# Token scales of a chunk transposed into one PSUM bank and copied once, two steps ahead of their use

## The chip, the cores and the metric

The kernel runs on one core of a Trainium2 chip. Five engines work at once and meet at semaphores: TensorE (matmuls and transposes, called PE in the profile, its weight loads PEld), VectorE (DVE), ScalarE (ACT), GpSimd (POOL) and SyncE (SP, which issues DMAs). Each engine runs its own instructions strictly in the order in which they were placed. The metric is device time in microseconds (us) of one execution.

## The reference, cut to what matters

Three layers follow each other: an attention with 32 memory slots, a mixture of 8 experts with two experts per token, and a dense layer over 2304 tokens of width 512. Only the last one and the sum of the two experts in front of it are touched here:

```
x = top2_w[:,0] * y_expert0 + top2_w[:,1] * y_expert1      # 2304 x 512
h = x @ w_in            # 512 -> 2048
g = h * cos(h)
out = g @ w_out         # 2048 -> 512
```

The kernel computes in pairs of fp16 numbers (a high part and the remainder), so each product is three matmuls: high by high, high by low, low by high. For that each token row of x is multiplied by a power of two of its own before it is split. The factor must be divided out again before the cosine, and there tokens stand along the free axis: the inverse scale of each token is therefore needed as a matrix in which every partition holds the same row of scales. That matrix is `bct`.

## The kernel before

The tokens are 18 tiles of 128. The last layer takes them in six chunks of 2, 2, 4, 4, 4 and 2 tiles (line 977). Each chunk has 16 steps, one for each block of 128 of the 2048 hidden columns; counted through, there are 96 steps, 0 to 95. The start of a chunk is called a border here: border 0 is step 0, border 1 step 16, border 2 step 32, and so on to border 5 at step 80.

What one step does (`m1`, lines 1047 to 1070): TensorE runs 12 matmuls into a bank `g` (line 1056 to 1058); VectorE scales the bank into `ty` with the scales `bct` (line 1064), and makes the argument of the sine in two further instructions (1065, 1066); ScalarE takes the sine (1067); VectorE multiplies it with the bank again (1068); ScalarE rounds that to fp16, the high part of `gT` (1069); GpSimd forms the low part (1070). `m2_` (line 1072) then multiplies `gT` with `w_out`, three steps after (`LAG = 3`): after the `g` matmuls of step u, TensorE runs the `o` matmuls of step u-3. The `g` banks are three in number (`bank_g`), so the matmuls of step u+1 need the bank that line 1068 of step u-2 has read for the last time.

What happens to a token tile t before its chunk (`comb`, line 986): two gathers by GpSimd fetch the tile's expert outputs, ScalarE and VectorE sum them, VectorE finds the largest magnitude (`mx`, tile `cmx`, line 1002), six instructions of one column follow, and ScalarE and VectorE write the two fp16 parts `chl`; a transposing DMA puts them into `x2T`. The inverse scale lies in column 2 of `cmx`. `cmx` has four buffers.

`c_bct` (line 1013) turns a tile's column of scales into rows: TensorE transposes the column, broadcast to 128 columns, into the PSUM bank `pb`, and ScalarE copies the 128 columns into `bct`. `pb` comes from `mbank`, which is one bank with one buffer, so the next tile's transpose waits until ScalarE has copied the one before.

The order of the work comes from two sources. Every piece is registered with a time by `at(...)`, and `issue` (line 95) turns the times into priorities; a scheduler that runs with a timeline of its own then places each instruction on its engine. Instructions recorded with `chain("P", ...)` keep the order in which they were recorded on TensorE. The copy of `c_bct` is not chained, so the scheduler places it on ScalarE among the sines and roundings. The times of the pieces in question are

```
        at(first[j] - 0.1 * (chunks[j][1] - t) - 1.0, c_bct, t)
```

that is, about 1 us before the chunk's first step, in the units of the plan.

Of the kernel before, what the change touches and what calls it, by code (L numbers as in the profile page):

```python
# [9 lines left out]
F32 = mybir.dt.float32  # L10
# [4 lines left out]
AF = mybir.ActivationFunctionType  # L15
# [4 lines left out]
P = 128  # L20
# [40 lines left out]
def fused_kernel(ctx, tc, phiT, qT, kv, wgn, noise, w1, w2, wi, wo, out):  # L61
    nc = tc.nc
    V, A, G, T, SP = nc.vector, nc.scalar, nc.gpsimd, nc.tensor, nc.sync
# [17 lines left out]
    def at(t, fn, *a, lead=None):  # L81
        line.append((t, len(line), fn, a, LEAD.get(fn.__name__, 0.0) if lead is None else lead))
# [18 lines left out]
    def l2k(shape, dt, name):  # L101
        return lp.tile(shape, dt, tag="l", name=name)


    def sm(shape, dt, name):
        return small.tile(shape, dt, name=name)
# [4 lines left out]
    ident = sm([P, P], F32, "ident")  # L111
# [39 lines left out]
    def pow2_scale(s, mx, tmp):  # L151

        V.tensor_scalar(tmp, mx.bitcast(I32), EXP_MASK, None, op0=OP.bitwise_and)
        V.tensor_scalar(tmp, tmp, float(TINY_BITS), -1.0, op0=OP.max, op1=OP.mult)
        V.tensor_scalar(s.bitcast(I32), tmp, float((3 + 253) << 23), None, op0=OP.add)

    def pow2_inv(r, s):
        V.tensor_scalar(r.bitcast(I32), s.bitcast(I32), -1.0, float(254 << 23), op0=OP.mult, op1=OP.add)
# [78 lines left out]
    def gated(key):  # L237

        return tc.issue_after(last[key].ins) if key in last else nullcontext()

    def chain(key, fn, *a, **kw):

        with gated(key):
            last[key] = fn(*a, **kw)  # L244
# [128 lines left out]
    def mbank(name):  # L373
        return bank("m", name)
# [437 lines left out]
    def mt(shape, dt, name, bufs=2):  # L812
        return pools["mp"].tile(shape, dt, tag=name, name=name, bufs=bufs)
# [162 lines left out]
    x2T, bct = {}, {}  # L976
    chunks = [(0, 2), (2, 4), (4, 8), (8, 12), (12, 16), (16, 18)]
    ch_of = {t: j for j, (a, b) in enumerate(chunks) for t in range(a, b)}

    cm = {}  # L980

    def c_place(t):
        j = ch_of[t]
        return j, slice((t - chunks[j][0]) * P, (t - chunks[j][0] + 1) * P)

    def comb(t):

        rows = min(YROWS, Y0 + (E - 1) * CAP + (t + 1) * P)
        y0, y1 = (l2k([P, DM], F32, f"y{k}") for k in range(2))
        for k, y in enumerate((y0, y1)):  # L990
            G.indirect_dma_start(out=y, out_offset=None, in_=yd[0:rows],
                                 in_offset=bass.IndirectOffsetOnAxis(ap=sidx[:, t, k:k + 1], axis=0))
        j, o = c_place(t)
        if t == chunks[j][0]:
            n = (chunks[j][1] - chunks[j][0]) * P
            x2T[j] = mt([P, 8, n], F16, "x2T")
            bct[j] = mt([P, n], F32, "bct")
        A.activation(y0, y0, AF.Copy, scale=cw[:, t, 0:1])
        V.scalar_tensor_tensor(y1, y1, cw[:, t, 1:2], y0, op0=OP.mult, op1=OP.add)
        mx = mt([P, 4], F32, "cmx", 4)  # L1000
        tmp = mt([P, 1], I32, "cmt")
        V.tensor_reduce(mx[:, 0:1], y1, axis=AX.X, op=OP.max, apply_absolute_value=True)
        pow2_scale(mx[:, 1:2], mx[:, 0:1], tmp)
        pow2_inv(ib[:, t:t + 1], mx[:, 1:2])
        V.tensor_scalar(mx[:, 2:3], ib[:, t:t + 1], 1.0 / (2.0 * math.pi), None, op0=OP.mult)
        V.tensor_tensor(osc[:, t:t + 1], ib[:, t:t + 1], ik, op=OP.mult)
        hl = l2k([P, 2, DM], F16, "chl")
        A.activation(hl[:, 0], y1, AF.Copy, scale=mx[:, 1:2])
        V.scalar_tensor_tensor(hl[:, 1], y1, mx[:, 1:2], hl[:, 0], op0=OP.mult, op1=OP.subtract)
        SP.dma_start_transpose(out=x2T[j][:, :, o], in_=hl.rearrange("p w d -> p (w d)"))  # L1010
        cm[t] = mx

    def c_bct(t):
        j, o = c_place(t)
        pb = mbank("pb")
        chain("P", T.transpose, pb[:, :P], cm.pop(t)[:, 2:3].to_broadcast([P, P]), ident)
        A.activation(bct[j][:, o], pb[:, :P], AF.Copy)  # L1017


    win, wout = [], []  # L1020
# [143 lines left out]
    first = {}  # L1164
    for u in range(len(units) + LAG):
        if u < len(units):
            j, f = units[u]
# [4 lines left out]
        if u >= LAG:  # L1172
            j, f = units[u - LAG]
# [3 lines left out]
    for j in range(2, len(chunks)):  # L1177
        a, b = chunks[j]
        y += [first[j - 1] + (first[j] - first[j - 1] - 20.0) / (b - a) * k for k in range(b - a)]
    for t in range(NT):  # L1180
        j = ch_of[t]
        at(y[t], comb, t)
        at(first[j] - 0.1 * (chunks[j][1] - t) - 1.0, c_bct, t)

    def next_table():
        chain("A", A.preload_act_table_set, "trig_and_small")
# [103 lines left out]
```

## Time and profile before

| what | value |
|---|---|
| median of three timed runs | 963.5 us (961.99 to 963.62) |
| the profiled execution | 956.12 us |
| its span, first to last instruction | 954.3 us |
| TensorE busy | 889.6 us (93%) |
| VectorE busy | 604.0 us (63%) |
| ScalarE busy | 467.3 us (49%) |
| GpSimd busy | 229.0 us (24%) |
| mean granted clock of TensorE | 0.971 |
| last layer (from border 0) | 558.9 us to the end |

The profile is one execution, recorded by the chip. A row of the timeline gives the start in us from the span's start, the duration, the engine, the line of the code (line 244 is the helper `chain`, so there one goes by the tile), the operation, the tiles written and read, the shapes, and in brackets how long the engine stood idle before it and what ended the wait. Matmuls overlap: a row's duration holds a tail that lies beside the next matmul, so the distance between starts says more than the duration. The shares of busy time are means over stages with different limits; what a change is worth must be read from the stage it touches.

### The profile page before, as it was taken

The page shows a single profiled execution, that of the slowest core. Times are in us where ns is not written, and L with a number is a line of the kernel's source. Part 1 is how long each engine was busy: PE and PEld are TensorE (multiplying, and loading weights), DVE is VectorE, ACT ScalarE, POOL GpSimd, SP SyncE. Part 2 cuts the span into 40 slices and gives each one's busy share as a digit, 9 for nine tenths or more (in the row PEclk, how much of TensorE's full clock was granted, in tenths as well). Part 3 has the DMA queues.
Part 4 walks back from the last instruction along what each step waited for, and adds up shares of the span by engine and source line. Part 5 has one row for each costly group of instructions (what it writes and reads, how often), then busy time and mean ns, then how long its engine had stood idle before and what let it go on. Part 6 is the DMA issues. An engine that isn't in the chain of part 4 may idle for free. (4 is left out here: it accounts for less than half of the span.)

```text
span 954.3 us, 14114 instructions
## 1 busy us (share of the span) xinstructions
PE 889.6 (93%) x5316; PEld 514.4 (54%) x5316; DVE 604.0 (63%) x1336; ACT 467.3 (49%) x826; POOL 229.0 (24%) x244
## 2 busy tenths in 40 slices
PE   5988179999999999999999999989999999999997
PEld 4756055564747565665746566654444444444564
DVE  4799781365866566676763458776855664555464
ACT  3575603566666666677782334443422532422242
POOL 1354831111110101011000134433421522221222
PEclk8997679999999999999999999999999999999999
DMA  9962219849887869988663363312300420200010
GB/s 355 399 255 77 78 49 271 271 159 287 273 238 252 210 263 291 282 243 314 226 188 134 100 223 76 97 37 64 91 1 12 122 44 1 78 12 1 1 45 22
DMA packets 108246, 146.54 MB, mean 154 GB/s; under 512 B 65808, under 2 KB 66448, under 8 KB 106128
## 3 DMA queue, kind: packets, MB, share of 16 engines
q1 hardware_dynamic: 89536, 103.56, 35.7%
q0 software_dynamic: 6080, 19.93, 7.2%
q10 hardware_dynamic: 12560, 22.13, 6.6%
q8 instruction: 42, 0.69, 0.3%
q14 instruction: 28, 0.23, 0.1%
HBM read 95.26 MB, written 35.13 MB: 137 GB/s over the span
## 5 line engine op out<-in xcount | busy, mean ns | idle before, releaser
L244 PE MATMUL g<-x2T,win 128*128 128x256 f16 (+1 forms) x1152 | 203.9, 327 | 0.0
L244 PE MATMUL o<-wout,gT 128*128 128x512 f16 x864 | 202.0, 379 | 0.3 <-ACT gT L1069 0.2
L244 PE MATMUL h<-x,w 128*128 128x384 f16 (+1 forms) x1440 | 201.6, 301 | 0.2 <-DVE hT L244 0.2
L244 PEld LDWEIGHTS <-w 128*128 128x128 f16 x1440 | 141.0, 99 | 56.8 <-issue 0.5
L244 PEld LDWEIGHTS <-win 128*128 128x128 f16 x1152 | 112.9, 98 | 84.0 <-issue 2.0
L1070 POOL TENSOR_TENSOR gT<-ty,gT 128x256 f16<-128x256 f32 (+1 forms) x96 | 92.0, 958 | 260.6 <-ACT gT L1069 260.4
L1067 ACT ACTIVATE tt<-tt,hp 128x256 f32<-128x256 f32 (+1 forms) x96 | 58.9, 614 | 174.8 <-DVE tt L1066 158.4
L244 PEld LDWEIGHTS <-gT 128*128 128x128 f16 x864 | 84.3, 98 | 93.1 <-ACT gT L1069 0.6
L914 PE MATMUL y<-w,hT 128*128 128x512 f16 x320 | 121.1, 379 | 2.1 <-issue 2.1
L912 PE MATMUL y<-w,hT 128*128 128x512 f16 x320 | 121.2, 379 | 0.0
L913 PE MATMUL y<-w,hT 128*128 128x512 f16 x320 | 121.1, 379 | 0.0
L1064 DVE SCALAR_TENSOR_TENSOR ty<-g,wis,bct 128x256 f32<-128x256 f32 (+1 forms) x96 | 58.9, 614 | 78.3 <-PE g L244 78.1
L244 DVE SCALAR_TENSOR_TENSOR hT<-h,hT 128x384 f16<-128x384 f32 (+1 forms) x128 | 61.3, 487 | 70.1 <-ACT hT L244 69.3
L244 ACT ACTIVATE hT<-h 128x384 f16<-128x384 f32 (+1 forms) x128 | 55.2, 435 | 88.7 <-PE h L244 56.4
L1068 DVE SCALAR_TENSOR_TENSOR ty<-g,fac,tt 128x256 f32<-128x256 f32 (+1 forms) x96 | 59.1, 615 | 51.0 <-ACT tt L1067 50.5
L244 DVE SCALAR_TENSOR_TENSOR w<-raw,wsc,w 128x1024 f16<-128x1024 f32 x56 | 70.8, 1280 | 32.0 <-ACT w L244 30.6
L1069 ACT ACTIVATE gT<-ty 128x256 f16<-128x256 f32 (+1 forms) x96 | 50.2, 523 | 59.1 <-DVE ty L1068 59.0
L851 POOL DMA_INDIRECT xg<-xd,idxB x24 | 24.9, 1036 | 222.9 <-DMA x<-xg 207.3
L1066 DVE SCALAR_TENSOR_TENSOR tt<-tt,ty 128x256 f32<-128x256 f32 (+1 forms) x96 | 64.7, 674 | 2.6
L244 ACT ACTIVATE w<-raw,wsc 128x1024 f16<-128x1024 f32 x56 | 62.5, 1139 | 2.2 <-ACT o L244 2.1
L244 ACT ACTIVATE o<-y,ysc 128x512 f32<-128x512 f32 x40 | 27.5, 686 | 70.5 <-PE y L914 70.5
L244 ACT ACTIVATE junk<-raw 128x1024 bf16<-128x1024 f32 x56 | 58.9, 1052 | 3.8 <-ACT o L244 2.9
(256 smaller groups left out, 945.1 us busy)
## 6 DMA issues: line engine op xcount, KB each, us to landing
raw<-in_w SPq DMA_DIRECT2D x32, 1024.0 KB
yd<-o ACTq DMA_DIRECT2D x40, 256.0 KB
kvt<-in_kv SPq DMA_DIRECT2D x9, 1024.0 KB
cvt<-in_wi SPq DMA_DIRECT2D x8, 1024.0 KB
wst<-cvt SPq DMA_DIRECT2D x16, 512.0 KB
cvt<-in_wo SPq DMA_DIRECT2D x8, 1024.0 KB
yd<-zero ACTq DMA_DIRECT2D x13, 512.0 KB
xd<-hl SPq DMA_DIRECT2D x18, 256.0 KB
```

The costliest lines, as they stand in the source:

```text
L244: last[key] = fn(*a, **kw)
L851: G.indirect_dma_start(out=g, out_offset=None, in_=xd[0:NA * P] if part == 0 else xd, in_offset=bass.IndirectOffsetOnAxis(ap=idx[:, col:co ...
L912: ins = [T.matmul(py, lhsT=hi[:, f, cs], rhs=w[:, 0, ws], start=(f == 0), stop=False), T.matmul(py, lhsT=hi[:, f, cs], rhs=w[:, 1, ws], st ...
L913: T.matmul(py, lhsT=hi[:, f, cs], rhs=w[:, 1, ws], start=False, stop=False),
L914: T.matmul(py, lhsT=lo[:, f, cs], rhs=w[:, 0, ws], start=False, stop=(f == 7))]
L1064: V.scalar_tensor_tensor(y, ph[:, :n], wis[:, 2 * E + c:2 * E + c + 1], bct[j], op0=OP.mult, op1=OP.mult)
L1066: V.scalar_tensor_tensor(t, t, MAGIC, y, op0=OP.subtract, op1=OP.subtract)
L1067: A.activation(t, t, AF.Sin, bias=hp, scale=-2.0 * math.pi)
L1068: V.scalar_tensor_tensor(y, ph[:, :n], fac[:, c:c + 1], t, op0=OP.mult, op1=OP.mult)
L1069: A.activation(g[:, 0, :n], y, AF.Copy)
L1070: G.tensor_tensor(g[:, 1, :n], y, g[:, 0, :n], op=OP.subtract)
```

## The change

The scales of a whole chunk go side by side into one `pb` bank (2 or 4 transposes of 128 columns), and one ScalarE instruction of 256 or 512 columns copies them. The work is registered once per chunk, at `first[j] - 5.3` in place of about `first[j] - 1.0`. `bct` is allocated there, at 512 columns, in place of in `comb` of the chunk's first tile; `cmx` has six buffers in place of four.

```
-            bct[j] = mt([P, n], F32, "bct")
...
-        mx = mt([P, 4], F32, "cmx", 4)
+        mx = mt([P, 4], F32, "cmx", 6)
...
-    def c_bct(t):
-        j, o = c_place(t)
+    def c_bct(j):
+
+        a, b = chunks[j]
         pb = mbank("pb")
-        chain("P", T.transpose, pb[:, :P], cm.pop(t)[:, 2:3].to_broadcast([P, P]), ident)
-        A.activation(bct[j][:, o], pb[:, :P], AF.Copy)
+        for t in range(a, b):
+            _, o = c_place(t)
+            chain("P", T.transpose, pb[:, o], cm.pop(t)[:, 2:3].to_broadcast([P, P]), ident)
+        bct[j] = mt([P, 512], F32, "bct")[:, :(b - a) * P]
+        A.activation(bct[j], pb[:, :(b - a) * P], AF.Copy)
...
-        at(first[j] - 0.1 * (chunks[j][1] - t) - 1.0, c_bct, t)
+        if t == chunks[j][1] - 1:
+            at(first[j] - 5.3, c_bct, j)
```

On TensorE at border 4 (step 64 starts a chunk of four tiles) the order before is: the end of step 60's `o` matmuls, four transposes, then the chunk's first `g` matmuls.

```order
L244 MATMUL o_7543<-wout_5800,gT_7874 128x512
L244 MATMUL pb_7996<-ident_73,cmx_7385 128x128
L244 MATMUL pb_7999<-ident_73,cmx_7518 128x128 [waits Activation_49]
L244 MATMUL pb_8002<-ident_73,cmx_7644 128x128 [waits Activation_49]
L244 MATMUL pb_8005<-ident_73,cmx_7766 128x128 [waits Activation_49]
L244 LDWEIGHTS win_4962 [waits DMAHW4_49,DMAHW5_49,DMAHW3_49,DMAHW2_49]
L244 MATMUL g_8008<-x2T_7381,win_4962 128x512 [waits DVE_49]
```

The same transposes in the changed kernel stand one step earlier, after step 59's `o` matmuls and ahead of step 63's `g` matmuls, which still read the chunk before (`x2T_6741`).

```order
L244 MATMUL o_7526<-wout_5797,gT_7701 128x512
L244 MATMUL pb_7945<-ident_73,cmx_7368 128x128 [waits PE_49]
L244 MATMUL pb_7945<-ident_73,cmx_7501 128x128
L244 MATMUL pb_7945<-ident_73,cmx_7627 128x128
L244 MATMUL pb_7945<-ident_73,cmx_7749 128x128
L244 LDWEIGHTS win_4964
L244 MATMUL g_7952<-x2T_6741,win_4964 128x512 [waits DVE_49]
```

The three waits on ScalarE inside the group are gone. The one wait that has come is on TensorE's own semaphore, for a matmul several hundred places before. In chunks of two tiles the group stands two steps ahead, since a step is shorter there; at border 0 it stands ahead of the last 24 `y` matmuls of the experts.

On ScalarE at the same border the copies stand before between the sine of step 63 (the row ahead of these), its rounding, the second half of a combined tile (`chl`) and the next sine.

```order
L1017 ACTIVATE bct_7382<-pb_7996 128x128 [waits PE_49]
L1017 ACTIVATE bct_7382<-pb_7999 128x128 [waits PE_49]
L1017 ACTIVATE bct_7382<-pb_8002 128x128 [waits PE_49]
L1069 ACTIVATE gT_7874<-ty_7975 128x512 [waits DVE_49]
L1008 ACTIVATE chl_8048<-y1_8032,cmx_8039 128x512 [waits DMAHW7_49,DVE_49]
L1017 ACTIVATE bct_7382<-pb_8005 128x128 [waits PE_49]
L1067 ACTIVATE tt_8022<-tt_8022,hp_98 128x512 [waits DVE_49,Activation_49]
```

In the changed kernel one copy of 512 columns stands between the sine and the rounding of step 62.

```order
L1070 ACTIVATE tt_7925<-tt_7925,hp_98 128x512 [waits DVE_49,Activation_49]
L1020 ACTIVATE bct_7950<-pb_7945 128x512 [waits PE_49]
L1072 ACTIVATE gT_7857<-ty_7924 128x512 [waits DVE_49]
L1070 ACTIVATE tt_7966<-tt_7966,hp_98 128x512 [waits DVE_49,Activation_49]
L1072 ACTIVATE gT_7857<-ty_7965 128x512 [waits DVE_49]
```

On VectorE at border 2 the search for the largest magnitude of tile 8 (`cmx_6755`) and what follows from it stand before inside step 31, the last of chunk 1, where it waits for a transpose to free one of the four `cmx` buffers.

```order
L1064 SCALAR_TENSOR_TENSOR ty_6697<-g_6684,wis_114,bct_5762 128x256 [waits PE_49,Pool_49]
L1002 TENSOR_REDUCE cmx_6755<-y1_6748 128x1 [waits PE_49]
L1065 TENSOR_SCALAR tt_6698<-ty_6697 128x256 [waits DVE_49]
L153 TENSOR_SCALAR cmt_6756<-cmx_6755 128x1 [waits DVE_49]
L1066 SCALAR_TENSOR_TENSOR tt_6698<-tt_6698,ty_6697 128x256 [waits DVE_49]
```

In the changed kernel steps 30 and 31 hold nothing but their own four instructions; those of tile 8 stand in steps 25 to 27 (at borders 3 and 4 the first tile of the chunk after next moves in the same way). In chunk 0 the four combined tiles each stand about one step later than before.

```order
L1067 SCALAR_TENSOR_TENSOR ty_6671<-g_6658,wis_114,bct_6112 128x256
L1068 TENSOR_SCALAR tt_6672<-ty_6671 128x256
L1069 SCALAR_TENSOR_TENSOR tt_6672<-tt_6672,ty_6671 128x256
L1071 SCALAR_TENSOR_TENSOR ty_6671<-g_6658,fac_159,tt_6672 128x256
L1067 SCALAR_TENSOR_TENSOR ty_6699<-g_6686,wis_114,bct_6112 128x256
L1068 TENSOR_SCALAR tt_6700<-ty_6699 128x256
```

The order of GpSimd differs by one place (one `gT` stands ahead of the second tile's gathers), that of SyncE not at all.

## Rows read from the trace of the kernel before

**Rows 1.** Who waited for whom in the last layer: total us, times, longest.

```profile
...
PE pb L244 <- ACT bct L1017: 10.0, 12, 2.2
...
```

**Rows 2.** Timeline of TensorE at border 0.

```profile
...
557.59 0.27 PE L244 MATMUL pb<-ident,cmx 128*128 128x128 f32 x1
...
558.86 0.38 PE L244 MATMUL g<-x2T,win 128*128 128x256 f16 x2
```

**Rows 3.** Timeline of all engines at border 1.

```profile
...
596.73 0.77 DVE L1066 SCALAR_TENSOR_TENSOR tt<-tt,ty 128x256 f32<-128x256 f32 x1
596.80 0.27 PE L244 MATMUL pb<-ident,cmx 128*128 128x128 f32 x1
...
598.98 0.26 ACT L1017 ACTIVATE bct<-pb 128x128 f32<-128x128 f32 x1
...
599.45 1.47 PE L244 MATMUL g<-x2T,win 128*128 128x256 f16 x12
...
```

**Rows 4.** Timeline of TensorE at border 2, and its next step.

```profile
...
639.83 0.27 PE L244 MATMUL pb<-ident,cmx 128*128 128x128 f32 x1
639.94 1.46 PE L244 MATMUL o<-wout,gT 128*128 128x512 f16 x6
...
646.35 4.11 PE L244 MATMUL g<-x2T,win 128*128 128x512 f16 x12
...
650.30 1.46 PE L244 MATMUL o<-wout,gT 128*128 128x512 f16 x6
...
651.59 2.75 PE L244 MATMUL g<-x2T,win 128*128 128x512 f16 x12
...
```

**Rows 5.** Busy time by stretch; PEclk, DMA share and GB/s stand last.

```profile
...
646.00:647.00 1.00, 0.91 (x3) 0.57 (x4) 0.66 (x1) 0.61 (x3) 0.58 (x1) 0.50 0.00 0
...
```

**Rows 6.** Timeline of TensorE at borders 3, 4 and 5.

```profile
...
726.70 0.27 PE L244 MATMUL pb<-ident,cmx 128*128 128x128 f32 x1
...
729.23 1.02 PE L244 MATMUL g<-x2T,win 128*128 128x512 f16 x4
...
812.11 0.27 PE L244 MATMUL pb<-ident,cmx 128*128 128x128 f32 x1
...
814.35 1.02 PE L244 MATMUL g<-x2T,win 128*128 128x512 f16 x4
...
897.23 0.27 PE L244 MATMUL pb<-ident,cmx 128*128 128x128 f32 x1
...
898.04 1.15 PE L244 MATMUL g<-x2T,win 128*128 128x256 f16 x9
```

**Rows 7.** Six fp32 transposes behind each other, in the attention stage (TensorE timeline).

```profile
...
47.47 0.82 PE L625 MATMUL et<-ident,ew 128*128 128x128 f32 x6
...
```

**Rows 8.** Timeline of VectorE: steps 0, 16, 28, 31, and one of chunk 3.

```profile
...
560.45 0.48 DVE L1064 SCALAR_TENSOR_TENSOR ty<-g,wis,bct 128x256 f32<-128x256 f32 x1 [15.47 <-PE g L244]
...
601.18 0.47 DVE L1064 SCALAR_TENSOR_TENSOR ty<-g,wis,bct 128x256 f32<-128x256 f32 x1
...
634.82 0.48 DVE L1064 SCALAR_TENSOR_TENSOR ty<-g,wis,bct 128x256 f32<-128x256 f32 x1
...
637.06 0.48 DVE L1068 SCALAR_TENSOR_TENSOR ty<-g,fac,tt 128x256 f32<-128x256 f32 x1 [0.64 <-ACT tt L1067]
...
642.77 0.48 DVE L1064 SCALAR_TENSOR_TENSOR ty<-g,wis,bct 128x256 f32<-128x256 f32 x1
...
804.61 0.75 DVE L1064 SCALAR_TENSOR_TENSOR ty<-g,wis,bct 128x512 f32<-128x512 f32 x1 [1.64 <-PE g L244]
...
```

**Rows 9.** Busy time by stretch: the sum over 578 to 600 us.

```profile
...
sum 22.00, PE 19.78 PEld 13.24 DVE 18.54 ACT 9.66 POOL 9.34; mean PE 0.90 PEld 0.60 DVE 0.84 ACT 0.44 POOL 0.42
```

**Rows 10.** Timeline of VectorE: tile 8's search, one of six small instructions, its last.

```profile
...
643.16 0.68 DVE L1002 TENSOR_REDUCE cmx<-y 128x1 f32<-128x512 f32 x1
...
644.57 0.15 DVE L154 TENSOR_SCALAR cmt<-cmt 128x1 int32<-128x1 int32 x1
...
645.91 0.75 DVE L1009 SCALAR_TENSOR_TENSOR chl<-y,cmx,chl 128x512 f16<-128x512 f32 x1
...
```

## The prediction

> **What bounds the kernel now.** I read the chain of waits first: in the last layer it runs almost wholly through TensorE's `g` and `o` matmuls, so what stops TensorE there costs its full length. The list of who waited for whom then names the stops: TensorE's transposes `pb` waited 12 times for ScalarE's copies `bct` [rows 1]. Twelve is what the code gives: 18 transposes, of which the first of each of the six chunks finds the bank free. The timelines at the six borders show how long each stop is from the first transpose to the chunk's first `g` matmul, which is more than the waits alone.
>
> Border 0: from 557.59 to 558.86, 1.27 us [rows 2]. Border 1: from 596.80 to 599.45, 2.65 us; the reader is to see that the first copy starts only at 598.98, since ScalarE had the sine of a late step ahead of it, whose argument VectorE was still forming at 596.73 [rows 3]. Border 2: the first transpose stands one step ahead and delays the `o` matmuls by 0.11 us; six `o` matmuls take 1.29 us (650.30 to 651.59), so TensorE is free at 641.23 and the `g` matmuls start at 646.35: 5.12 us, and 5.23 in all [rows 4]. After that stop the granted clock is 0.50, the lower of TensorE's two levels (1.2 GHz) [rows 5], and the first twelve matmuls take 4.11 us where the next twelve of their kind take 2.75: 1.36 us more [rows 4]. Borders 3, 4 and 5: 2.53, 2.24 and 0.81 us [rows 6].
>
> **The change part by part.** *The copies between transposes go.* What stays is 2 or 4 transposes behind each other. Six of the same shape and type took 0.82 us in the attention stage [rows 7]; with the 0.27 of a single one [rows 2] that is (0.82 - 0.27) / 5 = 0.11 us for each further one, the same 0.11 as between the transpose at 639.83 and the matmul behind it [rows 4]. So 0.22 us stay at a border of two tiles and 0.44 at one of four. The gain of TensorE, if nothing else holds it:
>
> border 0: 1.27 - 0.22 = 1.05; border 1: 2.65 - 0.22 = 2.43; border 2: 5.23 - 0.44 + 1.36 = 6.15; border 3: 2.53 - 0.44 = 2.09; border 4: 2.24 - 0.44 = 1.80; border 5: 0.81 - 0.22 = 0.59. Sum 14.1 us.
>
> The Trainium skill, page "TensorE: Matmul & The Clock Gate", section "Part 4: PE-mode transpose", prices a 128x128 transpose in a kernel's context at about 275 ns. By that the 18 would cost 18 x 0.275 = 4.95 us in place of 1.98, and the gain would be 3.0 us smaller all through; the row of this kernel, six in 0.82 us, speaks against it.
>
> *The wait for the tile scales.* The transposes now stand two steps (5.2 us) or one long step ahead, and `g` matmuls of the old chunk are queued behind them; were a `cmx` late, TensorE would stop there. The trace shows no transpose that waited for VectorE at the old place; the last tile of a chunk is combined steps before. I take 0; each late tile would cost its lateness, at most the 5.2 us by which the place moved.
>
> *The wider copy.* ScalarE runs 6 copies in place of 18 of 0.26 us [rows 3]. In chunks of four it stands between a sine and a rounding, where ScalarE waits for VectorE anyway. Cost 0; uncovered it would be about four times 0.26, 1 us a border, on a rounding that TensorE needs three steps later.
>
> *Six `cmx` buffers.* The search of tile 8 no longer stands in step 31 but in steps 25 to 27. In chunks of four tiles VectorE waits 1.64 us for TensorE in each step [rows 8], so at borders 3 and 4 the same shift is covered. In the chunks of two it is not, and this is the term that decides.
>
> *What is late next: VectorE in chunks 0 and 1.* A step there is 1.31 + 1.29 = 2.60 us on TensorE (twelve `g` matmuls: the 1.47 us of rows 3 less a tail of 0.16; then six `o`). VectorE needs (642.77 - 634.82) / 3 = 2.65 us for a step without any combining, since each holds a wait of 0.64 us for the sine [rows 8], and more with it. So it falls behind: step 31 is read at 642.77, 2.94 us after its matmuls ended at 639.83 [rows 4, 8]. The stops at borders 0 and 1 let it catch up; without them its delay is carried on. How far it may lag: the matmuls of step u+1 start 1.29 us after those of step u end and need the bank of step u-2, which is free 637.06 + 0.48 - 634.82 = 2.72 us after VectorE begins that step [rows 8]. So 2 x 2.60 + 1.29 - 2.72 = 3.77 us is the most.
>
> Now its own time. Step 0 can start 1.05 us earlier, at 559.40. From step 0 to step 16 it took 601.18 - 560.45 = 40.73 us [rows 8]. The same work stands there after the change, each combined tile one step later. VectorE was idle for 22.00 - 18.54 = 3.46 us of 578 to 600 [rows 9]; in the new order three steps of chunk 0 keep nothing to fill their 0.64 us, which is 1.92. So between 39.2 and 40.7 us; I take 40.0, the middle, as neither end has a nearer row. From step 16 to 31 it took 41.59 us; tile 8 adds 0.68 + 6 x 0.15 + 0.75 = 2.33 us [rows 10], of which one or two of the 0.64 us waits swallow part: 42.6 to 43.3 us, and I take 43.0. VectorE then begins step 31 at 559.4 + 40.0 + 43.0 = 642.4 (641.2 to 643.4). TensorE, unhindered, ends step 31's matmuls at 639.83 - 1.05 - 2.43 = 636.35, and VectorE may begin them at 640.12 at the latest. The difference of 2.3 us (1.1 to 3.3) is what TensorE must wait in small pieces within chunks 0 and 1. Behind border 2 VectorE has its 1.64 us in each step again, and nothing further is lost or won back. In chunk 5 VectorE sets the pace again, but it begins that chunk waiting for TensorE, so an earlier border moves the whole tail.
>
> The sum: 14.1 - 2.3 = 11.8 us, from 956.1 of the profiled execution to 944.3. The timed runs lie at 963.5, 7.4 us above it; nothing of that difference is known to lie at the borders, so I take the same 11.8 off: 951.7.
>
> **The rivals.** *The full gain.* VectorE's waits in chunks 0 and 1 shrink as the order changes, and TensorE is never held: 963.5 - 14.1 = 949.4. For it: the 3.46 us of idle time in one piece of chunk 0. Against: 2.65 is above 2.60 even in steps without combining.
>
> *The copies only hide VectorE's delay*, so the change does not do what it says at borders 1 and 2: VectorE comes later than reckoned, by tile 8's work and gathers that arrive late, and TensorE waits for it inside the chunks instead. Then borders 0, 3, 4 and 5 pay alone, 1.05 + 2.09 + 1.80 + 0.59 = 5.5 us: 958.0. For it: VectorE's row at 596.73 stands ahead of border 1's copy. Against: 3.77 us of allowed lag is more than the 2.94 it had, and the low clock after border 2 goes in any case.
>
> *Slower.* The one copy waits on ScalarE for transposes that TensorE reaches only behind the `o` matmuls of three steps ago; the rounding and the next sine are queued behind it, and VectorE waits for the sine. A hold of at most one step at each border, 5.18 us at three borders and 2.60 at three, would be 23.3 us, and 963.5 - 14.1 + 23.3 = 972.7; from 14.1 / 6 = 2.4 us a border on, the kernel is slower. For it: the copy's place between sine and rounding. Against: by then the sine has had to wait for that step's own matmuls and for VectorE, about as long as TensorE needs for the `o` matmuls and the transposes, and where VectorE lags, TensorE has long passed them.
>
> **How the numbers follow.** The forecast (11.8, its own range by the bounds 10.8 to 13.0, thus 950.5 to 952.7) has 0.55; the full gain 0.15; the second rival, from 958.0 down to what the forecast leaves, 0.22; no change, because something not seen holds each border, 0.05; slower 0.03. The range reaches from 948.8, a little below the full gain, to 956.0, which leaves out about half of the second rival and the last two. A change below 0.2% (1.9 us) cannot be told from none. Faster by more 0.92, within 0.05, slower 0.03.
>
> **What would show it.** Right: at each border the transposes follow each other within 0.5 us and the `g` matmuls come without a stop; no stretch behind border 2 has a granted clock of 0.50; TensorE waits for VectorE or for `gT` in chunk 1, 1 to 3 us in all. Wrong: if TensorE waits more than 4 us in chunks 0 and 1, the second rival holds; if ScalarE's copies wait over 1 us for the transposes and sines come later, the third; if no wait shows in chunk 1, the give-back was not there. Transposes of 0.25 us each would make the residue wrong.

## The result, and the profile after

| | median, us | executions | ratio to before |
|---|---|---|---|
| before | 962.75 | 961.11 to 963.62 | |
| changed | 953.42 | 952.41 to 954.13 | 0.9904 [0.9886, 0.9923] |
| changed, in a later group of runs (before there 960.47) | 950.90 | 950.62 to 953.12 | 0.9895 [0.9874, 0.9916] |

The gain is 9.3 and 9.6 us where 11.8 were forecast. The time lies within the range, 1.7 us above the forecast and outside the forecast's own narrow range (950.5 to 952.7).

The two profiled executions (956.12 before, 953.89 after) lie only 2.2 us apart, because the first trace of before was faster than all of its timed runs. A second trace of each kernel was therefore taken (962.26 and 951.13 us). The table gives the distance from the start of one named group of `o` matmuls to the next, read from TensorE's timelines: the first `o` matmuls of all, then those right behind the first `g` matmuls of chunks 1 to 5, and the last.

| stretch, us | before | before, again | changed | changed, again |
|---|---|---|---|---|
| last `y` row to first `g` (border 0) | 1.49 | 1.49 | 0.22 | 0.22 |
| chunk 0 and border 1 | 36.52 | 39.77 | 38.28 | 37.31 |
| chunk 1 and border 2 | 49.54 | 52.10 | 50.17 | 48.35 |
| chunk 2 and border 3 | 81.52 | 81.52 | 79.43 | 79.43 |
| chunk 3 and border 4 | 85.12 | 85.12 | 83.32 | 83.32 |
| chunk 4 and border 5 | 82.41 | 82.41 | 81.81 | 81.82 |
| chunk 5 | 42.96 | 42.96 | 42.97 | 42.96 |

TensorE is busy for 889.4 us (93%) in the changed kernel's first trace, VectorE 605.9 (64%), ScalarE 466.3 (49%), GpSimd 231.4 (24%), nearly as before. From chunk 2 on each kernel repeats itself to 0.01 us; what differs between executions of one kernel lies in chunks 0 and 1 (5.8 of the 6.2 us by which the two spans of before differ). Borders 3 to 5 give 2.09, 1.80 and 0.60 us.

The timeline of TensorE in the first trace of the changed kernel, at borders 0, 1 and 2, which answers to [rows 2 to 4] (start us, us, engine, line, operation, tiles, shapes, count):

```profile
553.32 0.38 PE L244 MATMUL pb<-ident,cmx 128*128 128x128 f32 x2
553.54 0.38 PE L912 MATMUL y<-w,hT 128*128 128x512 f16 x1
...
595.31 0.38 PE L244 MATMUL pb<-ident,cmx 128*128 128x128 f32 x2
595.52 1.47 PE L244 MATMUL g<-x2T,win 128*128 128x256 f16 x12
...
644.32 0.60 PE L244 MATMUL pb<-ident,cmx 128*128 128x128 f32 x4
644.76 1.47 PE L244 MATMUL g<-x2T,win 128*128 128x256 f16 x12
```

Two transposes take 0.22 us and four 0.44, and no row waits. The wait of [rows 1] is gone; in its place in the list of waits of the changed kernel stand TensorE's `g` matmuls waiting for VectorE's last read of the bank (total us, times, longest), and 0.4 us that ScalarE's copies wait for transposes:

```profile
PE g L244 <- DVE ty L1071: 6.5, 4, 3.4
```

```profile
ACT bct L1020 <- PE pb L244: 0.4, 2, 0.2
```

The timeline of all engines in the changed kernel's first trace shows the two large ones, ahead of steps 12 and 22 counted from step 0 (the expectations further down call them steps 11 and 20; in brackets: idle before, and what ended it):

```profile
581.28 1.25 POOL L991 DMA_INDIRECT y<-yd,sidx  x1 [0.31 <-issue]
581.74 1.23 SPq L1009 DMA_TRANSPOSE x2T<-chl  x1
...
588.45 0.75 DVE L998 SCALAR_TENSOR_TENSOR y<-y,cw,y 128x512 f32<-128x512 f32 x1 [3.98 <-DMA y<-yd,sidx]
...
589.64 1.47 PE L244 MATMUL g<-x2T,win 128*128 128x256 f16 x12 [2.72 <-DVE ty L1071]
...
613.20 0.97 POOL L991 DMA_INDIRECT y<-yd,sidx  x1 [0.15 <-issue]
...
618.97 0.72 ACT L997 ACTIVATE y<-y,cw 128x512 f32<-128x512 f32 x1 [4.12 <-DMA y<-yd,sidx]
...
620.66 2.72 PE L244 MATMUL g<-x2T,win 128*128 128x256 f16 x12 [3.43 <-DVE ty L1071]
```

Tile 4's second gather is issued at 581.28, half a microsecond ahead of tile 3's transposing DMA; VectorE adds its rows only at 588.45, and TensorE, which needs a bank that VectorE reads behind that, stops until 589.64. Tile 6 repeats this with ScalarE waiting. Behind that second stop the granted clock falls to 0.50, the lower level, as it did behind border 2 before [rows 5] (busy time by stretch; PEclk, DMA share, GB/s last):

```profile
622.00:625.00 3.00, 3.00 (x12) 1.48 (x11) 3.00 (x11) 1.75 (x4) 2.00 (x3) 0.50 0.34 91
```

The second trace has both stops too, 1.69 and 1.98 us, and behind the second of them the granted clock is 0.50 again (619 to 621 us).

### The profile page after: what moved, and what is told of

The parts are those of the page before. It is cut to its first block, busy times and chain, and to the rows that moved or that the text cites. A ratio compares the mean times of both kernels' runs of the same rounds, so it can differ in the third digit from the quotient of the medians.

```text
span 952.1 us, 14100 instructions
## 1 busy us (share of the span) xinstructions
PE 889.4 (93%) x5316; PEld 514.4 (54%) x5316; DVE 605.9 (64%) x1336; ACT 466.3 (49%) x814; POOL 231.4 (24%) x244
## 3 DMA queue, kind: packets, MB, share of 16 engines
q1 hardware_dynamic: 89536, 103.56, 35.4%
```

## The experiments

Each group of runs has a chip of its own and is set against the median of before there: 961.19 us for the first three rows, 961.33 for the next four, 960.47 for the last four. Chunks 0 and 1 are measured as in the table above, in one trace of each kernel.

| run | median, us | ratio | chunk 0 | chunk 1 |
|---|---|---|---|---|
| early_tiles | 964.81 | 1.0033 [1.0020, 1.0046] | 44.18 | 50.53 |
| merge_late | 950.29 | 0.9881 [0.9864, 0.9898] | 35.65 | 49.84 |
| comb_early | 951.02 | 0.9883 [0.9864, 0.9902] | 35.19 | 46.98 |
| late0 | 948.60 | 0.9868 [0.9846, 0.9889] | 35.40 | 49.03 |
| early0 | 950.66 | 0.9892 [0.9872, 0.9913] | 38.49 | 46.26 |
| late_cmx4 | 948.70 | 0.9861 [0.9840, 0.9881] | 35.04 | 47.94 |
| stores_sp | 949.15 | 0.9873 [0.9853, 0.9894] | 35.54 | 48.80 |
| after_again | 950.90 | 0.9895 [0.9874, 0.9916] | 37.31 | 48.35 |
| cmx4 | 950.39 | 0.9882 [0.9862, 0.9902] | 37.54 | 48.52 |
| plain3 | 948.99 | 0.9874 [0.9854, 0.9895] | 35.32 | 48.27 |
| tile6_late | 948.85 | 0.9870 [0.9847, 0.9893] | 35.58 | 47.65 |

**Where before's own executions differ.**

> The kernel before, unchanged, for a second trace: the first one was taken in an execution of 956.1 us, while the timed executions lie at 961 to 963.6. Theory (late gathers): the usual execution loses its extra 5 to 7 us in chunks 0 and 1, where some gathers of token rows land 5 us or more after their issue and VectorE and then TensorE wait for them; from the first g matmul of step 0 to that of step 32 it takes 91 us or more, where the first trace had 87.5. Rival (elsewhere): that stretch is 87 to 88.5 us again, and the extra time lies in the attention, expert or later stages.

From the first `g` matmul of step 0 to that of step 32 this one execution took 92.5 us (87.5 in the first trace), so the extra time is where the theory put it. Its cause shows in one gather: tile 3's second one is issued at 570.77, and VectorE's wait for its rows ends at 576.16, 5.4 us later. In the first trace that gather is issued at 570.43 and its rows are added at 574.15 without a wait. The timelines of GpSimd and VectorE, then of TensorE in chunk 0 and at border 1, and the busy time behind border 1:

```profile
570.77 0.95 POOL L991 DMA_INDIRECT y<-yd,sidx  x1 [0.30 <-issue]
...
576.16 0.75 DVE L999 SCALAR_TENSOR_TENSOR y<-y,cw,y 128x512 f32<-128x512 f32 x1 [1.78 <-DMA y<-yd,sidx]
```

```profile
596.18 1.47 PE L244 MATMUL g<-x2T,win 128*128 128x256 f16 x12 [1.13 <-DVE ty L1068]
...
601.52 0.48 PE L244 MATMUL pb<-ident,cmx 128*128 128x128 f32 x1 [2.47 <-ACT bct L1017]
601.79 2.77 PE L244 MATMUL g<-x2T,win 128*128 128x256 f16 x12
```

```profile
602.00:604.00 2.00, 2.00 (x12) 1.43 (x10) 0.86 (x2) 1.09 (x3) 0.10 (x1) 0.50 0.00 0
```

So TensorE waits for VectorE inside the chunks in the kernel before as well, 1.1 us in one place. And behind border 1's stop the granted clock is 0.50 here, the lower level, where the first trace has 1.00 (600 to 604 us). By the starts of TensorE's rows, some 2.4 of the 5.8 us come from the lower clock behind borders 1 and 2, 0.5 from longer stops at these borders and 2.9 from waits and small gaps within the chunks.

**Place or merging.** early_tiles keeps a bank and a copy for each tile and moves them alone; merge_late merges alone (both have the six `cmx` buffers):

```
-            at(first[j] - 5.3, c_bct, j)
+        at(first[j] - 0.1 * (chunks[j][1] - t) - 5.2, c_bct, t)   # early_tiles, c_bct per tile
+            at(first[j] - 1.1, c_bct, j)                          # merge_late
```

> The new place alone: the transposes stand two steps (one long step) ahead of the border as after the change, but each still has a bank and a copy by ScalarE of its own; six cmx buffers. Theory (the merging carries the gain): 12 transposes still wait for ScalarE, 10 us in all in the waits of TensorE on bct, so 960 to 963 us. Rival (the place carries it, since the copies there stand ahead of no late sine): the waits fall below 4 us and the time comes to 957 or less.

> The merging alone: the transposes of a chunk side by side in one bank and one copy, but at the old place, right ahead of the chunk's first g matmul; six cmx buffers. Theory (the merging carries the gain): TensorE has no wait for bct, the stops at the borders go as in the changed kernel, 952.5 to 954.5 us. Rival (the place matters as well): the copy now ends late for VectorE's first product of the new chunk or stands ahead of a rounding, TensorE stops 1 us or more in the step behind a border, and the time is 957 or more.

The place alone makes it 0.3% slower, the merging alone 1.2% faster: the merging carries the whole gain. In the list of waits of early_tiles the twelve waits are all there, and longer than in [rows 1]:

```profile
PE pb L244 <- ACT bct L1017: 12.0, 12, 3.5
```

merge_late came out under its theory's span (952.5 to 954.5), and below the changed kernel, but the intervals of the two ratios overlap: that the early place costs something is only suggested here.

**What the early place costs.** The schedule of the changed kernel differs from merge_late's in chunk 0 too: ScalarE scales tile 3 ahead of the sine of step 6 instead of behind it.

```
-            at(first[j] - 5.3, c_bct, j)
+            at(first[j] - (5.3 if j else 1.1), c_bct, j)   # late0
+            at(first[j] - (1.1 if j else 5.3), c_bct, j)   # early0
```

> The changed kernel with the transposes and copy of chunk 0 alone back at the old place (right ahead of step 0); those of the other five chunks stay two steps ahead. Merging at the old place everywhere took 950.3 us, the changed kernel 953.4. In the trace of the changed kernel ScalarE scales tile 3 ahead of the sine of step 6 and waits 1.36 us for its gather; with the merging at the old place it does so behind that sine. Theory (border 0's place turns this order, and with it tile 4's gather comes to be issued beside tile 3's transposing DMA): 949.8 to 951.3 us, and TensorE's stop of 2.7 us at step 11 falls below 1. Rival (the early place costs at borders 1 and 2, by transposes that delay the o matmuls or a copy ahead of a sine): 952.5 to 954.2.

> The mirror of the one before: the transposes and copy of chunk 0 alone two steps ahead, those of the other five chunks at the old place. Theory (border 0's place turns ScalarE's order in chunk 0): 952.5 to 954.2 us with a stop of over 2 us at step 11. Rival (the early place costs at borders 1 and 2): 949.8 to 951.3.

ScalarE, first in late0 and then in early0:

```profile
576.06 0.72 ACT L997 ACTIVATE y<-y,cw 128x512 f32<-128x512 f32 x1
```

```profile
575.31 0.72 ACT L997 ACTIVATE y<-y,cw 128x512 f32<-128x512 f32 x1 [1.30 <-DMA y<-yd,sidx]
```

The longest stop of TensorE in chunk 0 in the same two, ahead of step 10 in late0 (whose step 12 starts without one) and of step 12 in early0:

```profile
581.86 1.47 PE L244 MATMUL g<-x2T,win 128*128 128x256 f16 x12 [0.56 <-DVE ty L1071]
```

```profile
589.28 2.51 PE L244 MATMUL g<-x2T,win 128*128 128x256 f16 x12 [2.32 <-DVE ty L1071]
```

The order and the stop follow border 0's place, and chunk 0 takes 35.4 against 38.5 us. The times do not follow as neatly: late0 is 1.2 us under its theory's span, early0 1.8 under its own and inside its rival's. early0's chunk 1 was 2.8 us faster in its trace, which nearly makes up for the 3.1 us of chunk 0 there; the medians differ by 2.1 us, and the intervals touch.

**What makes tile 4's rows late.**

```
+        if t == 3:
+            SP.dma_start(x2T[j][:, :, o], hl.rearrange("p w (k d) -> p (w k) d", d=P))
+        else:
             SP.dma_start_transpose(...)
```

> The changed kernel with tile 3's transposing DMA turned into a plain one of the same 256 KB between the same tiles, from the same place in the same queue (tile 3 is then not transposed, so the outputs of its 128 tokens are others). Theory (tile 4's gather takes 7.1 us because it moves beside a transposing DMA): it lands within 4.5 us, the stop of 2.7 us at step 11 falls below 1.2, and the time is 1.2 to 3 us under the changed kernel beside it. Rival (any 256 KB beside a gather does that, or the gather is late by itself): the gather takes 5.5 us or more and the time is within 0.8 us of the changed kernel's.

From the scaling of tile 3 to the combining of tile 4 its order on the engines is the changed kernel's. The timeline of all engines in plain3:

```profile
581.17 1.25 POOL L991 DMA_INDIRECT y<-yd,sidx  x1 [0.30 <-issue]
581.63 0.71 SPq L1010 DMA_DIRECT2D x2T<-chl  x1
...
585.35 0.75 DVE L998 SCALAR_TENSOR_TENSOR y<-y,cw,y 128x512 f32<-128x512 f32 x1 [0.99 <-DMA y<-yd,sidx]
```

From the gather's issue to the adding it takes 4.2 us (585.35 - 581.17) instead of 7.2 in the changed kernel and 6.2 in its second trace; the stop ahead of step 12 is gone, chunk 0 is as fast as in late0, and the median is 1.9 us under the changed kernel's beside it, though the intervals of the ratios overlap. So the transposing DMA beside the gather is the cause of this stop. Such a neighbour does not always cost as much: in late0 tile 2's transposing DMA is issued 0.24 us behind tile 3's second gather, and that one lands after 4.7 us.

> The changed kernel itself once more, on the chip and against the executions of before that the next three share, so that these are compared with it directly. In its first trace TensorE stopped 2.72 us at step 11 and 3.43 us at step 20 for VectorE, which waited for gathers. If those late gathers belong to the kernel and not to that one execution, both stops show again (each over 1.5 us) and the time is 0.989 to 0.9925 of before; if not, it comes to 0.987 or less.

Both stops came again, 1.69 and 1.98 us, with a ratio of 0.9895: they belong to the kernel, as the first of the two cases says.

**Tile 6, and VectorE's own work in chunk 1.** stores_sp merges at the old place and takes chunk 0's stores from beside tile 6's gathers; late_cmx4 and cmx4 give back the two `cmx` buffers at the old and the new place; tile6_late is late_cmx4 with tile 6's work held behind step 20; comb_early is the changed kernel with tile 2 registered ahead of step 0, by which tiles 2 to 5 are combined one place earlier.

```
+        if t == 6:                                   # stores_sp
+            for u in range(2):
+                at(y[t] + 0.01, store, u)            # SP, chained behind tile 6's transposing DMA
-        mx = mt([P, 4], F32, "cmx", 6)
+        mx = mt([P, 4], F32, "cmx", 4)               # late_cmx4, cmx4
+        with gated("M") if t == 6 else nullcontext():   # tile6_late, and "S" for ScalarE
             V.scalar_tensor_tensor(y1, y1, ...)
-    y = [...] + [m0 + 3.0, m0 + 6.0]
+    y = [...] + [m0 - 1.0, m0 + 6.0]                 # comb_early
```

> The merging at the old place (950.3 us) with the two stores of chunk 0's output moved from ScalarE's queue at step 18 to SyncE's queue behind tile 6's transposing DMA, so that they no longer stand beside tile 6's gathers; tile 6's to 8's combining on VectorE comes out up to half a step later or earlier. Theory (those stores make tile 6's gather land 5.8 us after its issue, and VectorE and TensorE wait 3.5 us for it): the gather lands within 4 us, the stop at the start of chunk 1 goes with the half clock behind it, and the time is 945.5 to 947.5. Rival (VectorE's own lag takes the place of the stop): TensorE waits as long elsewhere in chunk 1, 949.5 to 951. Second rival (the stores now delay tile 7's gather instead): a stop of 2 us or more two to four steps later, 948 to 950.

The stop shrank from 3.46 us in merge_late to 2.74 only, so the theory's sign did not come. The gathers themselves came sooner without the stores (landing after 3.5 and 4.3 us, against 5.5 and 4.8 in late0), but the schedule had put the combining half a step earlier: VectorE wanted the second one's rows 1.9 us after its issue and waited 2.40 us, while no gather of this trace landed in under 3.2. So the test is blurred; the time (949.15) lies between theory and rival, within the second rival's span, but its sign, a stop of 2 us or more two to four steps later, is not there (the next long stop is 1.78 us, five steps later).

```profile
616.52 1.47 PE L244 MATMUL g<-x2T,win 128*128 128x256 f16 x12 [2.74 <-DVE ty L1071]
```

> The merging at the old place with four cmx buffers (948.7 us), and the scaling and adding of tile 6 held behind the sine and the second product of step 20, one to two steps later than they stood; its gathers stay where they were, those of tiles 7 and 8 come one step later. Theory (ScalarE and VectorE reach tile 6 before its rows have landed and hold the steps queued behind it): the stops of TensorE in chunk 1, 3.3 us in the two longest of late_cmx4, fall below 1.5, and the time is 945.5 to 947.3. Rival (VectorE has too little time in chunk 1 wherever the work stands): the stops move to later steps, within 0.8 us of 948.7.

The rival holds (948.85): TensorE's stop in the steps of tile 6 falls to 0.99 us, but there is one of 2.04 ahead of step 28, in the steps of tile 8:

```profile
633.56 1.47 PE L244 MATMUL g<-x2T,win 128*128 128x256 f16 x12 [2.04 <-DVE ty L1073]
```

> The merging at the old place (950.3 us) with four cmx buffers instead of six: the search and scales of tile 8 stand in step 31 again, as before the change, not in steps 25 to 27. Theory (VectorE has little to spare in chunk 1, so tile 8's 2.3 us of work there cost TensorE up to as much): 948.0 to 949.3. Rival (that work fits into waits of VectorE, and only late gathers hold TensorE): within 0.8 us of 950.3.

> The changed kernel with four cmx buffers instead of six: tile 8's search and scales stand in steps 29 and 30, not in 25 to 27, and those of one tile stand one chunk border later in the chunks of four. Theory (that work, 2.3 us of VectorE, costs TensorE in chunk 1): 1 to 2 us less than the changed kernel beside it; at the old place the same edit gave 950.3 against 948.7, intervals touching. Rival (no share of it): within 0.8 us of the changed kernel.

At the old place four buffers are 1.6 us faster than merge_late of another group, inside the theory's span; at the new place 0.5, inside the rival's; both with overlapping intervals. A share of the six buffers is not shown.

> The changed kernel with the combining of tiles 2 to 5 begun one tile earlier (tile 2 ahead of step 0, its gathers and all that follow a place earlier; the last place in chunk 0 stays empty). Theory (TensorE's waits in chunks 0 and 1 come from late gathers): tile 4's rows are there when VectorE wants them, the stop of 2.7 us at step 11 goes, and the time is 949 to 951.5 us. Rival (VectorE's own work holds TensorE): the 2.3 us of work ahead of step 0 only move the wait, 952.5 to 954.5. Second rival (ScalarE's scaling of tile 2 waits for its gather with the first sine queued behind it): 955 or more, with a stop of TensorE at steps 3 to 5.

The stop ahead of step 12 went, as the theory says, but the first `o` matmuls came 5.0 us later (569.12 against 564.11 in the changed kernel), since ScalarE waited for tile 2's rows ahead of the first sine, the second rival's mechanism. Chunks 0 and 1 won that back: 951.02, inside the theory's span.

The fastest versions, late_cmx4 and late0, lie 12.6 and 12.7 us under before of their group; the changed kernel lies 9.6 under before of its later group, and the intervals overlap.

## Why the prediction was right, and where it was not

*The borders.* Right in mechanism and size. Borders 3, 4 and 5 were forecast at 2.09, 1.80 and 0.59 and gave 2.09, 1.80 and 0.60. Border 0 gives 1.27 less the 0.22 that its transposes now take ahead of the last `y` matmuls: the 1.05 forecast.

*The residue.* 0.11 us for each transpose. The Trainium skill, page "TensorE: Matmul & The Clock Gate", section "Part 4: PE-mode transpose", gives about 275 ns; the trace has 273 ns for the duration of each of the 18, but behind each other they cost 0.11, and the distance decides.

*The wait for the scales and the wider copy.* No transpose waits, and the copies wait 0.4 us in all: 0, as forecast.

*The low clock behind border 2.* Gone there, but it comes back behind tile 6's stop in both traces (0.50 at 622 to 625 and at 619 to 621 us) and costs 2.8 and 1.7 us there, by the starts of the matmuls. So the 1.36 us were not won in either trace.

*What is late next: VectorE in chunks 0 and 1.* This is the step that failed, by its size. The forecast let TensorE lose 2.3 us there (1.1 to 3.3). Without any loss the two chunks with their borders would have taken 77.5 us (86.06 of the first trace of before, less 2.43 and 6.15); they took 85.66 in the second trace of the changed kernel and 88.45 in the first, so the loss was 8.2 and 11.0. The frame held: a step without combining takes 2.65 us (648.26 to 650.91 in the changed kernel), and VectorE lags by the reckoned limit. In the second trace it begins step 16 at 604.93, 3.75 us after that step's matmuls ended at 601.18; the limit was 3.77. But its own time was put at 40.0 us from step 0 to 16 and 43.0 from 16 to 31, and took 44.9 and 44.1. The rows of VectorE in that trace that open steps 0, 16 and 31, which answer to [rows 8]:

```profile
560.07 0.48 DVE L1067 SCALAR_TENSOR_TENSOR ty<-g,wis,bct 128x256 f32<-128x256 f32 x1 [14.60 <-PE g L244]
...
604.93 0.48 DVE L1067 SCALAR_TENSOR_TENSOR ty<-g,wis,bct 128x256 f32<-128x256 f32 x1
...
649.06 0.48 DVE L1067 SCALAR_TENSOR_TENSOR ty<-g,wis,bct 128x256 f32<-128x256 f32 x1
```

I took the durations from a trace in which hardly a gather was late, let "each combined tile one step later" cost nothing, and did not look at the DMA that the step moved the gather beside. plain3 shows what this neighbour is worth: without it VectorE takes 42.9 us from step 0 to 16, 2.0 less, and the median falls by 1.9. The other 2.9 us above the forecast's 40.0 stay. In plain3 VectorE still waits 1.0 us for a sine that stands on ScalarE behind a wait for tile 3's rows, and 1.0 for tile 4's; the rest is open. The kernel before, too, took 43.9 us in its second trace, where the forecast counted with 40.73.

*The base, and luck.* The 7.4 us between the first trace of before and its timed runs were taken as lying elsewhere than at the borders. In the second trace chunks 0 and 1 with borders 1 and 2 take 5.8 us more, and some 2.9 of these are at the borders: longer stops and the lower clock behind them. So two terms were wrong, and they offset each other: the loss in chunks 0 and 1 was put 6 to 9 us too small, and the kernel before, in its usual execution, was 5.8 us slower in the same stretch than the one I reckoned from. From that second trace the two chunks gain 6.2 us (91.87 - 85.66) against the second trace of the changed kernel and 3.4 against the first; the forecast was 2.43 + 6.15 - 2.3 = 6.3. From the first trace of before the same differences are 0.4 and -2.4. That the sum came so near is luck in this part; at borders 0, 3, 4 and 5 it is not.

*The rivals.* By the sign that I set for the second rival (TensorE waits over 4 us in chunks 0 and 1) both traces are past it: 6.7 and 5.1 us for VectorE, 0.2 and 1.1 of it put down to small instructions of the combining (`cmt`). In chunk 1 alone, where I looked for 1 to 3 us, they are 3.6 and 2.8. So by my own sign that rival holds. Its mechanism, gathers that arrive late and TensorE held inside the chunks instead, is there. Its price is not: it let borders 1 and 2 pay nothing and came to 958.0 us, and the medians are 953.42 and 950.90. The third did not come: the copies wait 0.4 us in all for transposes, under the 1 us of its sign. The waits of TensorE in the second trace:

```profile
PE g L244 <- DVE ty L1071: 4.0, 4, 2.0
...
PE g L244 <- DVE cmt L153: 1.1, 2, 0.6
```

*Left open:* what the 2.9 us within the chunks of the second trace of before consist of beyond tile 3's late gather, why that gather is late in one execution and not in the other, and what the rest of VectorE's 42.9 us from step 0 to 16 without the neighbour consists of.

## What to carry to other kernels

When a wait is removed by moving work, list the DMAs that now start together, not only the instructions: here one place in ScalarE's order put a gather beside a transposing DMA, and about 2 us were given back. Take two traces before sizing a stage whose waits depend on DMAs, and see which stretches repeat. When a sum comes out right, add up its parts again: here two wrong ones offset each other. And try the parts alone: the merging was worth all of it, and the earlier place without the merging made the kernel 0.3% slower.

## What the runs showed of the hardware

A gather of 256 KB that moves beside a transposing DMA of 256 KB took up to 7.1 us from issue to landing (6.1 in the second trace), against a median of 3.5 in the same trace; beside a plain DMA of the same tile the whole way to the adding took 4.2. The transposing DMA itself landed after 6.9 us, against a median of 3.1, and the plain one in its place after 4.5. In the first two microseconds below the DMA engines moved more bytes with the transposing DMA than without; in the next two they were no less busy, but moved far fewer. Busy time by stretch in the changed kernel, then in plain3:

```profile
582.00:584.00 2.00, 1.68 (x11) 0.78 (x10) 1.97 (x3) 1.06 (x2) 1.83 (x3) 1.00 1.17 179
584.00:586.00 2.00, 2.00 (x17) 1.50 (x16) 0.43 (x2) 0.58 (x2) 0.00 (x0) 1.00 0.86 75
```

```profile
582.00:584.00 2.00, 1.84 (x12) 0.88 (x10) 1.93 (x4) 1.14 (x2) 1.72 (x3) 1.00 0.59 143
584.00:586.00 2.00, 2.00 (x16) 1.47 (x15) 1.01 (x2) 0.51 (x1) 0.00 (x0) 1.00 0.77 207
```

A share of 0.86 carried 75 GB/s with the transposing DMA (118 in the second trace) and 0.77 carried 207 without. The Trainium skill, page "Advanced Engine Details and Errata", section "X-Bar Transpose (TRN2)", says that transposing DMAs are as fast as regular ones on this chip; for one of 256 KB beside a gather the 6.9 against 4.5 us differ from that, and they decide here.
